# Loading queries, keys and values uncast, casting them on GpSimd, and a values' copy in DRAM ordered by place within the chunk

## The chip, the cores and the metric

The kernel runs on one core of one Trainium2 chip. The metric is the device time of one execution in microseconds (us). TensorE is called PE, VectorE DVE, ScalarE ACT, GpSimd POOL and SyncE SP. POOL, SP and ACT also issue DMAs; all DMAs run on the same 16 engines.

## The reference

Two layers follow each other. The first is chunked attention over four batches of eight heads, 768 places and 64 columns; every chunk of 32 queries sees eight memory places and a span of 16 places before, 32 of and 8 after the chunk:

```python
for c in range(nc):
    l_start, r_end = max(0, c_start - 16), min(S, c_end + 8)
    k_full = np.concatenate([mem_k, k[:, :, l_start:r_end]], axis=2)
    v_full = np.concatenate([mem_v, v[:, :, l_start:r_end]], axis=2)
    scores = scale * np.matmul(q_c, k_full.transpose(0, 1, 3, 2))
    out[:, :, c_start:c_end] = np.matmul(softmax(scores), v_full)
```

The second is a mixture of eight experts over the 3072 rows of 512 columns: `logits + noise_scale * noise` picks two experts for each row, and the output is the weighted sum of `relu(x @ w1[e]) @ w2[e]` over these two.

## The kernel before, in words

**Attention.** A batch is 768 places, six groups of 128; a tile `t` is two groups, so there are three tiles to a batch and twelve in all (`NT`). The main loop runs over tiles `i`. Its engines' orders are written out by hand for PE, ACT, DVE and SP (`manual_schedule`); POOL's heavy instructions are held in program order by `pin`. For each tile the loop does: `scores(i+1)` (PE, L314), then DVE's maximum and subtraction (L340, L342); `turn_p(i)` (PE transposes the weights, ACT copies them, L351); `keep_x(i-1)` (ACT issues the store of a finished tile to DRAM, L405); `turn_x(i-1)` and `gate(i-1)` (L385, L394: the router's logits); `values(i)` (L360); `exps` on ACT (L345). `route` (L207) is a generator: it picks each row's two experts and their place in lists of rows by pair of experts, and its pieces are strewn over the loop, one batch behind; the last batch's routes stand after the loop (L480 to L495).

**Prefetch.** `load_nat` (L108) loads keys, values or queries of one batch with a DMA issued by POOL that casts fp32 to bf16 on its way. `turn` (L302) transposes keys or queries on PE, four units each; ACT and DVE copy them out (L425, L449, L466). Queries of the next batch are turned at the top of the last tile of a batch, keys in the tile before. Values are laid out by two POOL copies (`spread_v`, L284), written to DRAM in order of place, and read back as spans of the chunks (`window_v`, L290: SP issues one write, four reads in runs of 512 bytes and two copies of the memory's values). `await_v` (L416) is a POOL instruction that reads one value of the spans: whatever POOL issues next, the next batch's loads first of all, waits for the spans.

The large buffers of this stage (`xrow`, `vb`, `vp`, `vn`, `nat`) lie in the upper end of the room of the experts' weights (`scratch`, L96); experts 0 to 2 are loaded from tile 6 on, 3 and 4 after the first gathers.

**Experts.** POOL gathers rows from DRAM by the lists (`gather_x`, L534), PE transposes them (`transposes`, L548), and seventeen steps of `mm1` and `mm2` follow (L564, L579), a step for each expert and block of lists. Results are scattered to the output by POOL (`put`, L539).

The framework orders dependent instructions by semaphores. DMAs of SP and ACT share eight of them in turn: a DMA that takes one waits until the last DMA that used it has landed.

## Time and profile before

| | us |
|---|---|
| median of three runs | 411.07 |
| lowest and highest | 406.02, 411.64 |
| the profiled execution: its time | 413.39 |
| its span | 411.4 |
| PE busy | 314.9 (77%) |
| DVE busy | 174.5 (42%) |
| ACT busy | 120.3 (29%) |
| POOL busy | 102.6 (25%) |
| first use of values of batch 0 | 33.83 |
| spans landed, batches 0 to 3 (`await_v`) | 33.89, 67.75, 101.54, 133.80 |
| queries turned, batches 1 to 3 | 51.01, 86.05, 119.21 |
| first gather issued | 174.44 |
| first matmul of the experts | 184.28 |

Times of instructions are from the start of the span. Lines of the order of time give start and length in us, the engine, the line, operation, what is written and read with its shape, and in brackets how long the engine was idle before and what ended that; "issue" there means that nothing in the profile ended it. Lines of the waits give who waited for whom: us in total, how often, the longest. The slices cut the span in 40 equal parts and give busy tenths; PEclk is the granted clock of PE in tenths.

### The profile page before, as it was taken

The numbers are of one execution on the slowest core, as the hardware profiler recorded it, in microseconds if no ns is written. First come the engines' busy times: TensorE is split into PE (matmuls) and PEld (weight loads), VectorE is DVE, ScalarE is ACT, GpSimd is POOL, SyncE is SP. The second block draws the span as 40 slices with busy tenths as digits, with TensorE's granted clock in tenths as the row PEclk, the third lists the DMA queues.
The fourth block names the chain that finished last, engine by engine and source line by source line (L and its number), as shares of the span: only waits on it lengthen the run. The fifth ranks groups of instructions, "written<-read, shape, count | busy, mean of one in ns | idle before, by whom it ended". The sixth has DMA issues, their size and how long they took to land.

```text
span 411.4 us, 8936 instructions
## 1 busy us (share of the span) xinstructions
PE 314.9 (77%) x3841; PEld 203.2 (49%) x3862; DVE 174.5 (42%) x403; ACT 120.3 (29%) x182; POOL 102.6 (25%) x129
## 2 busy tenths in 40 slices
PE   1565394857748563149999999999999999999980
PEld 1444383746636453025555446665446765545530
DVE  1454053759767388832123321594321333112230
ACT  1222342523533332003432234312234222223300
POOL 5202202020120400074516532162250122100040
PEclk9999855555665555558999999999999999989996
DMA  9999994987999999739999970712130011100020
GB/s 129 206 142 102 197 180 71 221 191 116 191 195 157 158 218 222 124 91 177 191 196 246 238 172 14 116 42 90 48 92 1 23 65 45 48 1 3 19 79 31
DMA packets 50093, 49.85 MB, mean 121 GB/s; under 512 B 7064, under 2 KB 42968, under 8 KB 50049
## 3 DMA queue, kind: packets, MB, share of 16 engines
q0 software_dynamic: 28800, 36.32, 46.9%
q1 hardware_dynamic: 14112, 9.90, 12.2%
q10 hardware_dynamic: 7136, 3.02, 3.4%
q8 instruction: 32, 0.52, 0.5%
q14 instruction: 13, 0.10, 0.1%
HBM read 62.00 MB, written 13.96 MB: 185 GB/s over the span
## 4 chain that ended last, share of the span: by engine, by line
PE 52%; DVE 4%; issue 2%; POOL 1%; DMA 1%; POOLq 0%; ACT 0%
PE p_h L573 26%; PE p_y L582 24%; PE p_xt L554 1%; POOL xt L536 1%; DMA xt<-xd,main_src 1%; DVE vals L273 1%; DVE w_all L381 0%; PE p_list L277 0%; DVE facts L254 0%; DVE c L225 0%; DVE c L226 0%; POOLq L767 0%; DVE y L588 0%; DVE ii L227 0%; DVE mm L223 0%
## 5 line engine op out<-in xcount | busy, mean ns | idle before, releaser
L582 PE MATMUL p_y<-w_all,h 128*128 128x512 bf16 (+1 forms) x447 | 102.9, 382 | 1.1 <-issue 0.2
L573 PE MATMUL p_h<-xTt,w_all 128*128 128x384 bf16 (+2 forms) x636 | 102.3, 319 | 0.2
L573 PEld LDWEIGHTS <-w_all 128*128 128x128 bf16 (+1 forms) x704 | 68.3, 99 | 41.9 <-issue 2.7
L561 ACT ACTIVATE h<-p_h 128x512 bf16<-128x512 f32 (+1 forms) x82 | 44.7, 545 | 110.1 <-PE p_h L573 103.9
L559 DVE TENSOR_SCALAR h<-p_h 128x512 bf16<-128x512 f32 (+1 forms) x50 | 31.3, 626 | 93.8 <-PE p_h L573 79.3
L582 PEld LDWEIGHTS <-h 128*128 128x128 bf16 x464 | 45.2, 98 | 52.1 <-issue 1.7
L540 POOL DMA_INDIRECT out_dram<-y,main_dst x28 | 31.0, 1106 | 103.6 <-DVE y L588 89.3
L308 PE MATMUL p_t<-identb,w_all 128*64 128x128 bf16 x384 | 23.0, 313 | 27.8 <-DMA w_all<-in_q_dram 18.6
L588 DVE SCALAR_TENSOR_TENSOR y<-p_y,main_w,y 128x512 f32<-128x512 f32 x28 | 21.0, 750 | 37.4 <-PE p_y L582 32.3
L308 PEld LDWEIGHTS <-w_all 128*64 128x64 bf16 x384 | 20.5, 172 | 29.4 <-DMA w_all<-in_q_dram 19.2
L536 POOL DMA_INDIRECT xt<-xd,main_src x28 | 27.3, 975 | 29.4 <-PE p_xt L554 21.8
L330 PE MATMUL ps_s<-kT,qT 64*32 64x56 bf16 x768 | 24.1, 222 | 10.0 <-issue 10.0
L586 ACT ACTIVATE y<-p_y,main_w 128x512 f32<-128x512 f32 x28 | 19.2, 687 | 41.3 <-PE p_y L582 39.2
L357 ACT COPY pT<-p_p 128x1024 bf16<-128x1024 bf16 x12 | 12.1, 1012 | 50.9 <-PE p_p L354 50.9
L286 POOL COPY w_all<-w_all 128x1536 bf16<-128x1536 bf16 x8 | 11.5, 1466 | 39.0 <-DMA w_all<-in_v_dram 39.0
L323 PE MATMUL ps_s<-mkT,qT 64*128 64x8 bf16 x192 | 18.0, 185 | 2.9 <-DVE sc L342 2.9
L340 DVE TENSOR_REDUCE mx<-ps_s 128x16 f32<-128x1024 f32 x12 | 14.7, 1223 | 10.1 <-PE ps_s L330 9.8
L381 DVE TENSOR_TENSOR w_all<-ps_o,rs 128x512 bf16<-128x512 f32 x24 | 15.5, 686 | 5.9 <-PE ps_o L373 4.9
L417 POOL COPY seen<-w_all 128x1 bf16<-128x1 bf16 x4 | 0.8, 192 | 67.2 <-DMA w_all<-vd 67.2
L323 PEld LDWEIGHTS <-qT 64*128 64x128 bf16 x192 | 10.0, 101 | 13.3 <-issue 5.3
L554 PE MATMUL p_xt<-identb,xt 128*128 128x128 bf16 x116 | 10.6, 237 | 7.4 <-DMA xt<-xd,main_src 7.4
L373 PE MATMUL ps_o<-w_all,pT 64*32 64x64 bf16 x768 | 9.6, 229 | 7.8 <-issue 4.7
(156 smaller groups left out, 297.4 us busy)
## 6 DMA issues: line engine op xcount, KB each, us to landing
w_all<-in_moe_w_dram POOLq DMA_DIRECT2D x12, 1024.0 KB, 16.3
w_all<-in_moe_w_dram POOLq DMA_DIRECT2D x8, 512.0 KB, 7.9
w_all<-in_k_dram POOLq DMA_DIRECT2D x4, 768.0 KB, 8.3
w_all<-in_v_dram POOLq DMA_DIRECT2D x4, 768.0 KB, 12.0
w_all<-in_q_dram POOLq DMA_DIRECT2D x4, 768.0 KB, 15.1
vd<-w_all SPq DMA_DIRECT2D x4, 768.0 KB, 3.4
w_all<-vd SPq DMA_DIRECT2D x8, 384.0 KB, 8.8
xd<-w_all ACTq DMA_DIRECT2D x11, 256.0 KB, 6.6
```

The costliest lines, as they stand in the source:

```text
L308: nc.tensor.transpose(out=p_t[par * 64:par * 64 + 64, s, :], in_=src[:, 2 * pair + par, s * D:(s + 1) * D], identity=identb, tile_position ...
L323: nc.tensor.matmul(out=ps_s[:, par, j, pair, 0:NM], lhsT=q_[rows, pair, tk:tk + 128], rhs=mkT[rows, pair, b * NM:(b + 1) * NM], start=True ...
L330: nc.tensor.matmul(out=ps_s[r * CH:(r + 1) * CH, par, j, pair, NM:KW], lhsT=q_[rows, pair, tr:tr + CH], rhs=k_[rows, pair, tr:tr + WIN], s ...
L381: nc.vector.tensor_tensor(out=xr[:, j, 0:Dm].rearrange("p (c a d) -> p a c d", c=HP, a=2), in0=ps_o[:, :, j], in1=bc(rs[:, j].rearrange("p ...
L536: pin(nc.gpsimd.indirect_dma_start(out=xts[key].bitcast(I32), out_offset=None, in_=xd, in_offset=bass.IndirectOffsetOnAxis(ap=ix, axis=0)))
L540: i = nc.gpsimd.indirect_dma_start(out=out, out_offset=bass.IndirectOffsetOnAxis(ap=ix, axis=0), in_=y, in_offset=None, bounds_check=N - 1 ...
L559: nc.vector.tensor_scalar(out=out_, in0=in_, scalar1=0.0, scalar2=None, op0=Alu.max)
L561: nc.scalar.activation(out=out_, in_=in_, func=Act.Relu)
L573: nc.tensor.matmul(out=o, lhsT=w(kp * F + f * 128, 128), rhs=x[:, kp], start=(kp == 0), stop=(kp == KP - 1))
L582: nc.tensor.matmul(out=p, lhsT=h[:, (f * n + j) * 128:(f * n + j + 1) * 128], rhs=w(KP * F + f * Dm, Dm), start=(f == 0), stop=(f == FB - 1))
L586: nc.scalar.activation(out=y, in_=p, func=Act.Copy, scale=weight)
L588: nc.vector.scalar_tensor_tensor(out=y, in0=p, scalar=weight, in1=y, op0=Alu.mult, op1=Alu.add)
```

## The change

Queries, keys and values are loaded as fp32 (`fetch`), for the first batch by SP and for the others by POOL, and cast by copies: of batch 0 on ACT (keys), POOL and DVE (values) and DVE (queries), of later batches on POOL (`narrow`, `spread_v`). The values' copy in DRAM has one row for each place within the chunk, and in it all 24 chunks and a chunk of zeros on each side; it is written by eight DMAs (`away_v`), and a span is read by six DMAs in which each partition reads one run of 12 KB. `ahead(b)` puts a batch's casts, copies and the loads of the batch after in one sequence on POOL and SP, one batch earlier than before; `await_v` stays for batch 0 and the last. The copies of later batches' queries are all ACT's. The first small loads move from SP to ACT. `xrow` becomes three buffers of a tile. In the last two routes the chain of differences `d` runs on POOL, and the order of the pieces changes; `decode` moves into the hand-written part. The first expert starts after three gathered tiles; the other three are transposed behind its `mm1`.

```diff
-    xrow = [scratch(SO * Dm).rearrange("p (s r) -> p s r", s=SO) for _ in range(2)]
+    xrow = [scratch(2 * Dm).rearrange("p (s r) -> p s r", s=2) for _ in range(3)]
...
+    SV = 8
+    PV = S // SV
+    vp = scratch(H * SV * D)[0:PV]
+    k32, q32 = [scratch(2 * H * SO * D).bitcast(F32).rearrange("p (h c) -> p h c", h=H) for _ in range(2)]
+    v32 = scratch(2 * H * SV * D)[0:PV].bitcast(F32).rearrange("p (h c) -> p h c", h=H)
+    vd = [tc.dram_tile([2, CH, NCH + 2, HP * D], BF16, name=f"vd{i}") for i in range(2)]
+
+    def fetch(eng, x, b):
+        t, a, n = {"k": (k32, k, SO), "q": (q32, q, SO), "v": (v32, v, SV)}[x]
+        i = eng.dma_start(out=t, in_=a[b].rearrange("h (p s) d -> p h (s d)", s=n))
+        if eng is nc.gpsimd:
+            pin(i)
+
+    for x in "kvq":
+        fetch(nc.sync, x, 0)
...
     for i in range(2):
-        for r0, n in ((0, LC), (LC + S, CH - LC)):
-            nc.sync.dma_start(out=vd[i][r0:r0 + n, :], in_=zeros[0:n, :])
+        for x in range(2):
+            nc.scalar.dma_start(out=vd[i][x].rearrange("k c w -> k c w")[:, 0:NCH + 2:NCH + 1, :], in_=zeros[:, x])
-    nc.sync.dma_start(out=mks, in_=mem_k.rearrange("b h m d -> (b h m) d").rearrange("(x p) d -> p x d", p=128))
+    nc.scalar.dma_start(out=mks, in_=mem_k.rearrange("b h m d -> (b h m) d").rearrange("(x p) d -> p x d", p=128))
...
-    def route(g0, n, lg):
+    def route(g0, n, lg, eng=nc.vector):
...
-        nc.vector.tensor_tensor(out=d, in0=mm[:, 1], in1=mm[:, 0], op=Alu.subtract)
+        hold = pin if eng is nc.gpsimd else lambda m: m
+        hold(eng.tensor_tensor(out=d, in0=mm[:, 1], in1=mm[:, 0], op=Alu.subtract))
         for i in range(3):
-            nc.vector.tensor_copy(f_[:, :, 2 + i], d)
+            hold(eng.tensor_copy(f_[:, :, 2 + i], d))
...
+    def spread_v(engs=(nc.gpsimd, nc.gpsimd)):
+        for par, eng in enumerate(engs):
+            i = eng.tensor_copy(
+                out=vp.rearrange("p (s a c d) -> p a c s d", s=SV, a=2, c=HP)[:, par],
+                in_=v32.rearrange("p (c a) (s d) -> p a c s d", a=2, s=SV)[:, par])
...
+    def away_v(b):
+        src = vp.rearrange("p (s a w) -> p s a w", s=SV, a=2)
         for par in range(2):
+            for r in range(CH // SV):
+                nc.sync.dma_start(out=vd[b % 2][par, r * SV:(r + 1) * SV, 1:NCH + 1, :].rearrange("s c w -> c s w"),
+                                  in_=src[r:PV:CH // SV, :, par, :])
 
     def window_v(b):
         t, o = vb[b % 2], vd[b % 2]
-        nc.sync.dma_start(out=o[LC:LC + S, :].rearrange("(p s) c -> p (s c)", s=SO), in_=vp)
         for par in range(2):
...
+            for r0, n, c0, k0 in ((0, LC, 0, CH - LC), (LC, CH, 1, 0), (LC + CH, RC, 2, 0)):
+                nc.sync.dma_start(out=t[p0 + NM + r0:p0 + NM + r0 + n], in_=o[par, k0:k0 + n, c0:c0 + NCH, :])
             nc.sync.dma_start(out=t[p0:p0 + NM], in_=mvn[b * NM:(b + 1) * NM, cols].unsqueeze(1).to_broadcast([NM, NCH, 256]))
-            for r0, n in ((0, CH), (CH, WIN - CH)):
-                nc.sync.dma_start(out=t[p0 + NM + r0:p0 + NM + r0 + n],
-                                  in_=o[r0:r0 + S, cols].rearrange("(c k) w -> k c w", k=CH)[0:n])
+
+    def narrow(x, b):
+        pin(nc.gpsimd.tensor_copy(nat[b % 2][x], (k32, q32)[x]))
...
+    def ahead(b):
+        if b < B:
+            narrow(0, b)
+            if b + 1 < B:
+                fetch(nc.gpsimd, "k", b + 1)
+            spread_v()
+            away_v(b)
+            if b + 1 < B:
+                fetch(nc.gpsimd, "v", b + 1)
+            narrow(1, b)
+            if b + 1 < B:
+                fetch(nc.gpsimd, "q", b + 1)
...
-        spread_v(0)
+        for h in range(0, H, 4):
+            nc.scalar.copy(nat[0][0][:, h:h + 4], k32[:, h:h + 4])
+        fetch(nc.gpsimd, "k", 1)
+        spread_v((nc.gpsimd, nc.vector))
+        away_v(0)
         window_v(0)
+        for u in range(HP):
+            o_, i_ = turn(0, u)
+            nc.scalar.copy(o_, i_)
+        for h in range(0, H, 4):
+            nc.vector.tensor_copy(nat[0][1][:, h:h + 4], q32[:, h:h + 4])
         await_v(0)
-        for u in range(2 * HP):
+        fetch(nc.gpsimd, "v", 1)
+        fetch(nc.gpsimd, "q", 1)
+        for u in range(HP, 2 * HP):
...
         pbs[0] = exps(scores(0))
         nc.scalar.dma_start(out=nz, in_=moe_noise.rearrange("(g p) e -> p g e", p=128))
+        ahead(1)
         for i in range(NT):
             if tp == 0 and b + 1 < B:
                 window_v(b + 1)
-                await_v(b + 1)
-                if b + 2 < B:
-                    load_nat(nat[b % 2][0], k, b + 2)
-                    load_nat(vn, v, b + 2)
-                    load_nat(nat[b % 2][1], q, b + 2)
-                    spread_v(b + 2)
+                if b + 1 == B - 1:
+                    await_v(b + 1)
+                ahead(b + 2)
...
-                    (nc.scalar.copy if u % 2 else nc.vector.tensor_copy)(o_, i_)
+                    nc.scalar.copy(o_, i_)
...
-        ra = route(g0, SO - 2, lgs[B - 1][:, 0:SO - 2])
-        rb = route(g0 + SO - 2, 2, lgs[B - 1][:, SO - 2:SO])
+        ra = route(g0, SO - 2, lgs[B - 1][:, 0:SO - 2], nc.gpsimd)
+        rb = route(g0 + SO - 2, 2, lgs[B - 1][:, SO - 2:SO], nc.gpsimd)
...
-    for i in range(3):
-        turn_block(0, i)
+    turn_block(0, 0)
+    transposes(xTs[0], 2, blocks[0][0][2:3])
     dst, wl = next(dec)
...
         h = mm1(xTs[b][:, :, s0:s0 + (n - 1) * ds_ + 1:ds_, :], n, static_w(e), i % 2)
+        if i == 0:
+            transposes(xTs[0], 3, blocks[0][0][3:4])
+            turn_block(0, 2)
```

## The prediction

> **What bounds the kernel now.** I read the slices first, then the waits, then the order of time around one batch, then the chain.
>
> ```profile
> ## 2 busy tenths in 40 slices
> PE   1565394857748563149999999999999999999980
> PEclk9999855555665555558999999999999999989996
> DMA  9999994987999999739999970712130011100020
> ```
>
> Two stages stand here. From slice 18 (about 184 us) on, TensorE is at 9 with the clock near full: the mixture of experts, 216 us, bound by PE; among its waits from 184 to 400 us PE shows 0.2 us in all. The change leaves its matmuls alone. The first 184 us, attention, have PE at half busy and DMA at 9. So the question is what PE waits for there.
>
> ```profile
> POOL seen L417 <- DMA w_all<-vd: 67.2, 4, 17.7
> POOL w_all L286 <- DMA w_all<-in_v_dram: 39.0, 4, 11.3
> PE p_t L308 <- DMA w_all<-in_q_dram: 18.6, 4, 6.3
> PE ps_s L330 <- issue: 10.0, 2, 5.7
> ```
>
> GpSimd (POOL) holds the prefetch: it waits 67.2 us for the spans of the values, and only behind that issues the next batch's loads. PE pays with waits for queries. The order of time around batch 0 to 1 shows the loop:
>
> ```profile
> 33.83 0.73 PE L373 MATMUL ps_o<-w_all,pT 64*32 64x64 bf16 x63 [3.04 <-DMA w_all<-vd]
> 33.89 0.19 POOL L417 COPY seen<-w_all 128x1 bf16<-128x1 bf16 x1 [17.23 <-DMA w_all<-vd]
> 34.35 0.92 POOL L109 DMA_DIRECT2D w_all<-in_k_dram  x1 [0.26 <-issue]
> 41.63 2.77 PE L308 MATMUL p_t<-identb,w_all 128*64 128x128 bf16 x48 [1.55 <-DMA w_all<-in_k_dram]
> 47.16 2.87 POOL L286 COPY w_all<-w_all 128x1536 bf16<-128x1536 bf16 x2 [10.12 <-DMA w_all<-in_v_dram]
> 51.01 2.77 PE L308 MATMUL p_t<-identb,w_all 128*64 128x128 bf16 x48 [6.29 <-DMA w_all<-in_q_dram]
> 67.78 0.24 PE L330 MATMUL ps_s<-kT,qT 64*32 64x56 bf16 x6 [5.67 <-issue]
> 82.34 1.37 DVE L256 TENSOR_TENSOR d<-d,facts 128x6 f32<-128x6 f32 x1
> ...
> 85.18 0.17 DVE L256 TENSOR_TENSOR d<-d,facts 128x6 f32<-128x6 f32 x1
> ```
>
> The reader is to see: spans of batch 0 land at 33.8, loads go out at 34.35, keys are used 7.3 us, values 12.8 us, queries 16.7 us later. PE loses 6.29 us for the queries of batch 1, and 4.10 and 4.86 for those of batches 2 and 3 (at 86.05 and 119.21). The 5.67 us at 67.78 have no releaser and end as the span reads land (`seen` at 67.75); such a stall of 4.32 stands at 143.25. During plain loads it is smaller: 1.08 at 77.99.
>
> **The change part by part.** In the built program I followed which instruction waits for which. Durations are of the profiled execution (span 411.4, time 413.39, which is 2.3 above the median of the three runs, 411.07).
>
> 1. First batch, to the first use of values (33.83 before). The three loads go out on SP at about 0.8 in place of 1.35 on POOL, and land about 4.1 apart as before (9.50, 13.79, 17.62): keys 8.5 to 9, values 13. An uncast load is not in the trace; nearest rows: 3.4 us to landing for the uncast 768 KB `vd<-w_all`, and twice that, 6.8, for its 1536 KB; I take the cast load's 4.1 to 5.5, since it reads the same bytes. New: the small loads moved to ACT stand there ahead of the keys' cast, and one waits for the keys' landing: five issues of about 0.45 (rows of 0.37 to 0.54), then two ACT copies of 128x1536. 128x768 took 0.80 and 128x1024 1.01, so 1.43 each (bounds 1.01 and 2.0): done at 14. Then POOL issues keys of batch 1, which share the engines with the queries: queries at 20, keys(1) at 23. Queries are cast on DVE in two halves, 0.84 each by the two cast rows (128x128 0.25, 32x512 0.41; upper bound 1.6); PE turns them from 21, where before it was 17.62. The scores follow as before, so `exps(0)` starts 8.1 to 8.3 later, at 29.5 (25.70 before).
> The first of the eight copies of values to DRAM waits for keys(1), since the build holds it behind every uncast load ahead of it. It goes at 23, eight issues of 0.5 (rows 0.35 to 0.86), landed by 30; this is hidden, because in the middle of the span reads SP stands still: the copy of `mvn` there uses the semaphore of the noise load and waits for it, and ACT issues that load with `exps(0)` at 29.5. Its landing no row shows: between 2.8 (the gate's noise load) and 8.8 (a span read); I take 5, being 96 KB of short runs. Then five more issues (2.9) and 2.3 to land: 39.6. So the spans are there at 39.6, not 33.8: **+5.8**.
>
> 2. From there to the queries of batch 1 (17.1 us before). POOL order now: wait for spans, load v(1), load q(1), cast k(1), load k(2), two value casts, load v(2), cast q(1). The copies to DRAM wait for k(2), and v(2) waits for all eight copies; cast q(1) is queued behind v(2). So: three loads 17.5 (16.7 before, k(2) issued later); eight issues 4.0 (bounds 2.8 and 6.9); landing 2.5 (row 3.4 with its transfer); load issue 0.9; cast 2 x 1.44 = 2.9 by L286's 2.87 for the same 3072 elements (fp32 in place of bf16; up to 5.8); semaphores 0.4. 28.2, **+11.1**. PE turns these queries at 67.7, not 51.0: **+16.9** there. PE is then idle about 17 us, against 6.29.
>
> 3. What the later batches gain. Span reads in 12 KB runs queue less; I take both issue stalls down to the 1.08 seen during loads: **-4.6** and **-3.2** (bounds 0 and all). Queries(2) need k(3), eight copies and a cast behind them: ready near 97.4, when PE would be ready at 94; wait 3.3 for 4.10, and 0.89 of PE waiting for ACT's copy goes: **-1.7**. Queries(3) have no such copy ahead of their cast and come 10 us early: **-5.7** (4.86 and 0.89). Copies of queries moved from DVE to ACT cost nothing: PE turned keys with all four on ACT in 2.77 without a stall.
> Casts on POOL delay DVE: the operation at 82.34 took 1.37 while L286 ran, its like at 85.18, after it, 0.17. Two to five casts can meet `route`'s small operations: between 0 and 13 us, mostly while PE waits for queries anyhow; I take **+1.0**.
>
> 4. Tail. `route`'s d chain moves to POOL, whose queue holds only the six weight issues (4.9 us from 133.92, long done by 162.9): 12 operations of 0.15 to 0.18 leave DVE, in part covered by the PE wait beside them: **-1.0** (0 to 2.2). The first expert starts after three gathered tiles instead of six: third transposed by 180.5, matmuls at 181 not 184.28; twelve transposes then move behind it, 0.7: **-2.5** (bounds 0 and 3.2). Hidden: xrow of three buffers (a store lands in 6.6, three tiles last over 17), earlier scratch reuse by expert weights (they took 134 to 170, needed from 184), `decode` moved.
>
> Sum: 16.9 - 4.6 - 3.2 - 1.7 - 5.7 + 1.0 - 3.5 = -0.8. The profiled execution would take 412.6; against the median, 411.07 - 0.8 = 410.3.
>
> [...] From 90 to 103 us PE had no gap over 1.1 us and its granted clock stayed 0.50. [...]
>
> **The rivals.**
> Faster: the start-up chain is shorter than I make it. If uncast loads take 3.4 each, like the copy to DRAM, and the noise load doesn't hold SP, spans land at 35 and queries(1) come 22 later, at 57: +6 in place of +16.9, and the sum is -11.7, 399. For it: the spans are 112 runs of 12 KB in place of 2688 of 512 bytes (shapes of L298). Against it: 16.7 us for three loads was read-bound in the trace at the same bytes. It decides once queries(1) come before about 60.
> Slower, by loads: an uncast load writes twice the bytes; at 6.8 each the three loads take 21 to 23, keys(1) delay the start by 2 to 3, and queries(2) wait some 5 longer since k(3) gates them too: +11 to +13, 422. For it: the DMA row is at 9 throughout the first 18 slices. It decides once three loads take over 21 us after the spans.
> Slower, by the casts: each of the five POOL casts that can meet `route` holds a DVE operation to its end, on the path: 2.9+2.9+2.0+2.0+2.9, +11.7 over my 1.0, 422. [...] The trace agrees (1.37 and 1.40 for 0.17). Against it on the path: both hits before fell while PE waited for queries.
> The issue stalls stay as they are: +7.8, 418, still within 2%.
>
> **How the numbers follow.** Within 2% is 402.8 to 419.3, about what a measurement of this kernel can tell from no change. The forecast has 0.50 (0.12 of it for stalls that stay, 0.08 for the clock), and its own range is 403 to 418: the first step 3 either way by the noise load's bounds, the second 3 by the issues', the stalls up to 7.8. The short start-up has 0.31, slower by loads 0.13, by casts 0.06. I take a third of the faster case to lie below 397 and under half of the slower ones over 421, so 397 to 421 leaves out under 2 in 10. The time is that of the forecast, 410.3.
>
> **What would show it.** Spans' first use at 39.6 and an SP wait for noise: step 1. Queries(1) turned near 67.7, POOL's load of v(2) waiting for the copies to DRAM: step 2; if PE turns them before 60, that step is wrong. Stalls without a releaser under 2 us in the scores, waits for queries(2) and (3) of 3.3 and 0: step 3. A first `p_h` matmul after three gathers: step 4. The forecast falls if uncast loads are not 4 to 5.5 us, or if `route` on DVE stretches on PE's path.

## The result, and the profile after

The changed kernel takes 440.88 us (median of 4 executions, 440.37 to 441.12) beside 411.36 for the kernel before, measured with it (406.02 to 415.75). The ratio is 1.0763, with a 95% interval of 1.0661 to 1.0864: slower by 7.6%. Executions of before differ by up to 10 us: the ratio leaves out its slowest (415.75), and its profiled one took 413.39. The prediction was 410.3, its range 397 to 421. The profiled execution of the changed kernel spans 439.1 us, 27.7 more than the 411.4 of before.

The slices come first:

```profile
PE   0243250256674969522999999999999999999970
PEclk9999995565655575555799999999999999999995
DMA  8948495899698676999699997162121011100020
```

From slice 19 (about 209 us) on the stage of the experts looks as before. The loss is ahead of it. Of the first ten slices PE is at 2 or less in 0, 1, 4, 6 and 7, and DMA, which before stood at 9 in most slices of attention (4 in slice 6), is at 4 to 6 in several. DMA is not fuller than before. It waits too. The waits say for what (in total us, times, longest):

```profile
POOL seen L457 <- DMA w_all<-mvn: 56.6, 2, 34.7
...
POOL w_all L114 <- DMA vd<-w_all: 28.8, 2, 15.1
PE p_t L325 <- POOL w_all L316: 28.8, 2, 24.0
...
PE ps_o L390 <- issue: 16.1, 4, 7.3
```

The second and third line are one chain: the load of values(b+1) waits on POOL for the copies away, the cast of queries(b) stands behind it, and PE waits for the cast. The order of time through the first two batches (start, duration, instruction, idle time before it and what ended it):

```profile
25.14 6.57 SPq L303 DMA_DIRECT2D vd<-w_all  x8
31.83 1.27 SPq L312 DMA_DIRECT2D w_all<-vd  x3
40.89 0.76 SPq L313 DMA_DIRECT2D w_all<-mvn  x1
...
52.45 0.73 PE L390 MATMUL ps_o<-w_all,pT 64*32 64x64 bf16 x63 [6.29 <-DMA w_all<-mvn]
...
73.13 6.44 SPq L303 DMA_DIRECT2D vd<-w_all  x8
...
81.82 0.79 POOL L114 DMA_DIRECT2D w_all<-in_v_dram  x1 [15.11 <-DMA vd<-w_all]
82.60 2.75 POOL L316 CAST w_all<-w_all 128x3072 bf16<-128x3072 f32 x1
...
85.41 2.77 PE L325 MATMUL p_t<-identb,w_all 128*64 128x128 bf16 x48 [23.96 <-POOL w_all L316]
```

The reader is to see the hole of SP between 33.1 and 40.89, in the middle of the first span reads (its waits give 7.8 us for the noise load `nz`), and PE idle for 24 us until 85.41. The table sets the same points of both kernels side by side, from the orders of time; the points of the experiments follow below in the same columns.

| point | before | after | later by |
|---|---|---|---|
| first copies of values away, issued | 16.69 | 25.14 | 8.5 |
| first values on PE (spans of batch 0 there) | 33.83 | 52.45 | 18.6 |
| second copies away, issued | 50.06 | 73.13 | 23.1 |
| queries(1) turned on PE | 51.01 | 85.41 | 34.4 |
| last values on PE | 154.87 | 184.78 | 29.9 |
| first matmul of the experts | 184.07 | 209.96 | 25.9 |
| end of the span | 411.4 | 439.1 | 27.7 |

All that is lost is lost by queries(1). After that the batches come at the pace of before (copies away at 73.13, 110.40 and 142.37; before at 50.06, 85.14 and 118.01).

### The profile page after: what moved, and what is told of

Read it like the earlier page. It is cut to its first block, busy times and chain, and to the rows that moved or that the text cites. A ratio compares the mean times of both kernels' runs of the same rounds, so it can differ in the third digit from the quotient of the medians.

```text
span 439.1 us, 9020 instructions
## 1 busy us (share of the span) xinstructions
PE 310.4 (71%) x3862; PEld 199.8 (46%) x3862; DVE 167.5 (38%) x387; ACT 128.5 (29%) x192; POOL 121.5 (28%) x141
## 3 DMA queue, kind: packets, MB, share of 16 engines
q1 hardware_dynamic: 12032, 14.42, 15.6%
## 4 chain that ended last, share of the span: by engine, by line
PE 50%; DVE 3%; DMA 1%; POOL 1%; issue 0%; POOLq 0%; ACT 0%
PE p_h L608 25%; PE p_y L617 23%; PE p_xt L589 2%; DMA xt<-xd,main_src 1%; POOL xt L571 0%; DVE vals L280 0%; DVE w_all L398 0%; PE p_list L284 0%; DVE c L232 0%; DVE c L231 0%; POOLq L806 0%; DVE y L623 0%; DVE ii L233 0%; DVE mm L229 0%; DVE oh_l L278 0%
## 5 line engine op out<-in xcount | busy, mean ns | idle before, releaser
L325 PE MATMUL p_t<-identb,w_all 128*64 128x128 bf16 x384 | 20.4, 291 | 40.1 <-POOL w_all L316 28.8
L325 PEld LDWEIGHTS <-w_all 128*64 128x64 bf16 x384 | 18.4, 159 | 41.2 <-POOL w_all L316 28.9
L293 POOL CAST w_all<-w_all 96x2048 bf16<-96x2048 f32 x7 | 14.1, 2044 | 27.9 <-DMA w_all<-in_v_dram 27.9
L390 PEld LDWEIGHTS <-pT 64*32 64x32 bf16 x768 | 7.5, 105 | 23.1 <-issue 23.0
L508 ACT COPY qT<-p_t 128x768 bf16<-128x768 bf16 x12 | 8.8, 805 | 28.5 <-PE p_t L325 28.4
## 6 DMA issues: line engine op xcount, KB each, us to landing
w_all<-in_moe_w_dram POOLq DMA_DIRECT2D x12, 1024.0 KB, 16.2
```

What stands on the lines that cost most here:

```text
L325: nc.tensor.transpose(out=p_t[par * 64:par * 64 + 64, s, :], in_=src[:, 2 * pair + par, s * D:(s + 1) * D], identity=identb, tile_position ...
L390: nc.tensor.matmul(out=ps_o[r * CH:(r + 1) * CH, par, j, pair, :], lhsT=pT[rows, j * HP + pair, r * CH:(r + 1) * CH], rhs=vb[b % 2][rows, ...
```

## The experiments

The first theory was the chain just read: SP stops for the noise load, the reads in 12 KB runs land late, and the cast of queries(1) is stuck behind the copies. Its rivals were that the uncast loads are too much to move, and that the new order of the values' copy is slow by itself. The points of time of all runs, in us of the profiled executions (time is the median of all executions; first values are those that need both halves of the spans; the kernel before, run beside each group of experiments, had medians between 409.63 and 414.74, so times of different groups compare to about 1%, and the ratio is the better measure there):

| run | time | ratio to before (95%) | first values | queries(1) | first values of batch 1 | last values |
|---|---|---|---|---|---|---|
| before | 411.36 | 1 | 33.83 | 51.01 | 70.46 | 154.87 |
| after | 440.88 | 1.0763 (1.0661 to 1.0864) | 52.45 | 85.41 | 107.05 | 184.78 |
| e1 | 442.36 | 1.0777 (1.0663 to 1.0892) | 53.41 | 72.67 | 106.39 | 184.33 |
| e2 | 440.17 | 1.0743 (1.0595 to 1.0891) | 49.23 | 82.19 | 103.58 | 179.88 |
| e3 | 445.81 | 1.0848 (1.0706 to 1.0990) | 54.32 | 87.32 | 113.36 | 189.00 |
| e4 | 444.14 | 1.0798 (1.0648 to 1.0949) | 52.80 | 85.73 | 107.30 | 187.15 |
| e5 | 442.28 | 1.0715 (1.0582 to 1.0848) | 50.74 | 70.07 | 113.25 | 186.85 |
| e6 | 438.20 | 1.0625 (1.0495 to 1.0754) | 43.19 | 62.23 | 104.95 | 182.53 |
| e7 | 439.45 | 1.0680 (1.0545 to 1.0816) | 42.29 | 99.40 | 113.30 | 183.49 |
| e8 | 421.87 | 1.0239 (1.0114 to 1.0364) | 38.90 | 55.84 | 90.78 | 164.89 |
| e9 | 430.04 | 1.0398 (1.0343 to 1.0452) | 39.65 | 62.55 | 81.46 | 172.30 |
| e10 | 411.98 | 0.9960 (0.9907 to 1.0012) | 34.27 | 55.13 | 71.79 | 154.97 |
| e11 | 422.42 | 1.0180 (1.0101 to 1.0259) | 38.81 | 56.02 | 74.65 | 166.13 |
| e12 | 409.99 | 0.9906 (0.9850 to 0.9961) | 33.12 | 50.38 | 68.47 | 153.94 |
| e13 | 430.28 | 1.0541 (1.0460 to 1.0623) | 39.80 | 62.75 | 78.74 | 171.24 |
| e14 | 438.37 | no interval | 40.81 | 63.86 | 80.76 | 175.97 |
| e15 | 404.72 | 0.9861 (0.9803 to 0.9918) | 34.98 | 48.76 | 65.94 | 150.29 |
| e16 | 441.44 | 1.0815 (1.0725 to 1.0905) | 42.31 | 68.08 | 88.17 | 181.53 |
| e17 | 428.21 | 1.0483 (1.0389 to 1.0576) | 35.91 | 85.04 | 98.56 | 173.51 |
| e18 | 454.76 | 1.1074 (1.0954 to 1.1193) | 46.79 | 72.93 | 93.97 | 198.50 |

### The waits that the profile names, one by one

**e1: the cast of queries ahead of the load that waits.**

```diff
             spread_v()
+            narrow(1, b)
             away_v(b)
             if b + 1 < B:
                 fetch(nc.gpsimd, "v", b + 1)
-            narrow(1, b)
-            if b + 1 < B:
                 fetch(nc.gpsimd, "q", b + 1)
```

> The cast of queries(b) stands on POOL ahead of the issue of values(b+1), which waits for the eight copies away; nothing else is changed. Theory of the queue (POOL holds the cast of queries(1) at 82.60 although its load has landed with keys(2) by 73): the cast runs at about 73 to 76, queries(1) turn at about 76 instead of 85.41, the wait of 4.79 for queries(2) goes too, and the time is 427 to 432 (-9 to -14). Rival, the volume of the loads: the three uncast loads, 1.5 MB each, are what is late, the wait moves to the next of them, and the time is 438 to 441.

The wait was there and goes: queries(1) turn at 72.67, 12.7 us earlier. The time does not move (442.36). PE's own line says where the gain went:

```profile
72.67 2.77 PE L325 MATMUL p_t<-identb,w_all 128*64 128x128 bf16 x48 [10.00 <-POOL w_all L316]
...
106.39 0.74 PE L390 MATMUL ps_o<-w_all,pT 64*32 64x64 bf16 x63 [15.04 <-DMA w_all<-mvn]
```

Behind the wait for queries stood another of nearly the same end: the spans of batch 1 land at 106.39, where the changed kernel uses them at 107.05. The longest wait of PE was a cover over the chain of the values (load, spread, copies away, span reads), and that chain sets the pace.

**e2: the noise load issued at the start.**

```diff
     nz = const.tile([128, NG, E], F32, name="nz")
+    nc.scalar.dma_start(out=nz, in_=moe_noise.rearrange("(g p) e -> p g e", p=128))
...
-        nc.scalar.dma_start(out=nz, in_=moe_noise.rearrange("(g p) e -> p g e", p=128))
```

> The noise load is issued at the start, behind the memory keys and the gate's weights, instead of behind exps(0); nothing else is changed. Theory of the wait on SP (7.8 us in the middle of the first span reads): the second half of the reads is issued at about 34 instead of 41.76, the first values come at 44 to 46 instead of 52.45, and the time is 433 to 435. Rival, the reads themselves are slow, as 12 KB runs that land in 7 us: both halves run together and land at 49 or later, and the time is 437 to 441.

SP no longer stops, and the first values come 3.2 us earlier, at 49.23, not at 44 to 46. The rival holds: with nothing between them the reads, issued from 33.38 on, still take 15.9 us to the first use. Before, in runs of 512 bytes, they took 13.8 (20.06 to 33.83).

**e3: the same reads in runs of 512 bytes**, by padding each place's row.

```diff
-    vd = [tc.dram_tile([2, CH, NCH + 2, HP * D], BF16, name=f"vd{i}") for i in range(2)]
+    vd = [tc.dram_tile([2, CH, NCH + 2, HP * D + 32], BF16, name=f"vd{i}")[:, :, :, 0:HP * D] for i in range(2)]
```

> The values' DRAM copy keeps its order, but each place's row of chunks is padded by 32 elements, so that the same span reads go in runs of 512 bytes instead of 12 KB. Theory that the long runs are what lands late (45.21 to 52.45, about 7 us where before took 2.3): the last reads land in 2.5 to 3 us, the first values come at about 48, and the time is 435 to 437. Rival, the landing is the queue's and the volume's and not the run length's: no change, 440 to 441, or slower, 442 to 446, since the reads are 24 times as many packets.

445.81: the rival's slower side. The run length is not what lands late. The 2.3 of the theory stands in no row of before, either: there the first values were used 9.55 us after the last read was issued.

```profile
21.99 2.29 SPq L298 DMA_DIRECT2D w_all<-vd  x2
```

**e4: the small loads ahead of the three first loads in the program.**

```diff
-    for x in "kvq":
-        fetch(nc.sync, x, 0)
...
     nc.scalar.dma_start(out=wgs[:, :, E:2 * E], in_=moe_w_noise.rearrange("(kp p) e -> p kp e", p=128))
+    for x in "kvq":
+        fetch(nc.sync, x, 0)
```

> The small loads (zeros, memory keys and values, gate weights) stand ahead of the three first loads in the program, so that the load of queries(0) no longer waits for the memory keys; nothing else is changed. Theory that this wait (queries(0) issued at 12.10 instead of about 1.9) sets the start: copies away at about 20 to 22 instead of 25.14, queries(0) turned at about 20 instead of 25.65, the noise load 5 earlier, and the time is 434 to 437. Rival, the first 25 us are bound by the 6 MB of four uncast loads: copies still at 25, and the time is 439 to 441.

This run doesn't tell. The queries' load still went out at 12.01, so the wait that it was to remove stayed. What that wait costs is open.

### Which part of the change costs

**e5 and e6: the copies away without partition steps.** The eight copies read every fourth partition, and in the built program such a read waits for all three uncast loads ahead of it (SP's waits ahead of the copies of the changed kernel: 52.4 us in three stops for keys, 16.8 in two for queries, 14.3 in one for values). e5 keeps eight copies but reads neighbouring partitions; e6 makes one copy of each half.

```diff
-            for r in range(CH // SV):
-                nc.sync.dma_start(out=vd[b % 2][par, r * SV:(r + 1) * SV, 1:NCH + 1, :].rearrange("s c w -> c s w"),
-                                  in_=src[r:PV:CH // SV, :, par, :])
+            nc.sync.dma_start(out=vd[b % 2][par, :, 1:NCH + 1, :].rearrange("(r s) c w -> c r s w", s=SV),
+                              in_=src[:, :, par, :])
```

(This is e6; e5 has four of them in each half, over six chunks each.)

> Still eight copies away of the same bytes to the same places, but each reads 24 neighbouring partitions (six whole chunks) instead of every fourth partition. In the program the copies then wait only for the spread, no longer for the three uncast loads, and the load of values(b+1) waits only for the spread of values(b), no longer for the landing of the eight copies. Theory of these two waits as the loop that sets the pace (copies 73.13, values(2) issued 81.82, spread of it 101.82, copies 110.40): copies(1) go at about 67, values(2) is issued at about 67, queries(1) turn at about 73 instead of 85.41, copies(2) at about 90 instead of 110.40, and the time is 410 to 422. Rival, the volume of the uncast loads sets the pace whatever waits for what: 430 to 438. The first values stay at about 52 by both, since the noise load still stops SP.

> One copy away for each half, over all 96 partitions, instead of four: the same bytes and places, two issues instead of eight, and none of the waits named for the eight copies of whole rows. Theory of the waits and of the issue time (8 copies 6.4 to 7.4 us of SP): another 2 to 5 us below the eight copies of whole rows, 406 to 420. Rival, one copy lands later than four beside one another: the same as the eight or up to 5 us above.

Everything up to queries(1) comes earlier, in e6 by 23 us (62.23), and by the last values 2 us of it are left. Both times lie above what their theories allow, and e5's above its rival's too. Again the spans of batch 1 are late, at 104.95 in e6. SP's waits in e6:

```profile
SPq L311 <- DMA vd<-w_all: 46.6, 4, 16.8
...
SPq L311 <- DMA xd<-w_all: 23.7, 3, 8.9
```

Two things are in it. The span reads wait 46.6 us for the copies to land: freed from the loads, the copies now run beside three loads in flight, and what was issued at 55.74 has landed only at 75.11. And 23.7 us go to a transfer that the reads don't need, the store of finished rows `xd`. The DMAs of SP and ACT take eight semaphores in turn (in the trace of the changed kernel their issues carry the numbers 101 to 108, round and round), and here a read's number is one that a row store still holds. The changed kernel stops 0.9 us for `xd`. In e5 such stops sum to 21.4 us. So the theory that the waits of the copies set the pace falls: without them the copies meet the loads.

**e7 and e8: half of the change each, loads as early as in the changed kernel.** e7 has the casting loads of before with the new order; e8 the old order (one copy away, `mvn` ahead, two reads a half) with the fp32 loads and GpSimd's casts.

```diff
-        t, a, n = {"k": (k32, k, SO), "q": (q32, q, SO), "v": (v32, v, SV)}[x]
+        t, a, n = {"k": (nat[b % 2][0], k, SO), "q": (nat[b % 2][1], q, SO), "v": (v32, v, SV)}[x]
...
     def narrow(x, b):
-        pin(nc.gpsimd.tensor_copy(nat[b % 2][x], (k32, q32)[x]))
+        pass
```

```diff
+        nc.sync.dma_start(out=vd[b % 2][LC:LC + S, :].rearrange("(p s) c -> p (s c)", s=SV), in_=vp)
...
+            for r0, n in ((0, CH), (CH, WIN - CH)):
+                nc.sync.dma_start(out=t[p0 + NM + r0:p0 + NM + r0 + n],
+                                  in_=o[r0:r0 + S, cols].rearrange("(c k) w -> k c w", k=CH)[0:n])
```

> The order of the values' copy, the spans and the edits at the end are kept; the loads are again the casting ones on POOL, straight into the bf16 tiles, and the casts of keys and queries are gone. In the program the eight copies then wait for the spread alone, and so does the load of values(b+1). Theory of the waits: the loop of copies and loads is gone with them, 408 to 422, though the first spans still stop for the noise. Rival, the order of the copy (12 KB reads, eight copies, SP stopped) is what costs: 425 to 440.

> The loads in fp32, the casts on GpSimd and the edits at the end are kept; the values' copy in DRAM and the span reads are those of before (one copy away, runs of 512 bytes). In the program the copy away then waits for the spread alone and the load of values(b+1) likewise. Theory of the waits: 405 to 420. Rival, the uncast loads and their casts are what costs: 430 to 440.

e8 gives back 19.0 of the 29.5 us with the fp32 loads and casts still there. So the uncast loads are not the main cost; 421.87 is just above the range of its theory. e7 does not tell: it loads keys and queries of batch 3 over those of batch 1 before these are turned (there are two tiles, and the changed kernel had the fp32 tiles between), so batch 1 is computed with the wrong keys and queries, and PE waits for the later load.

**e9 to e12: four kernels of one design.** In all four the three loads of a batch are issued only behind POOL's wait for the spans of the batch before, as in the kernel before. This gate was dropped by the change for two of the batches.

```diff
-                if b + 1 == B - 1:
-                    await_v(b + 1)
+                await_v(b + 1)
+                for x in "kvq" if b + 2 < B else "":
+                    fetch(nc.gpsimd, x, b + 2)
                 ahead(b + 2)
```

The loads in `ahead` go, and keys(1) are loaded behind the first wait as well.

e9 has the new order (two copies) and fp32 loads, e10 the old order and fp32 loads, e11 the new order and casting loads, e12 the old order and casting loads.

> The new order with the two copies away, fp32 loads and casts, and now all three loads of a batch are issued only behind POOL's wait for the spans of the batch before, as before (keys(1) too, which had been issued at 13.6). Theory that the transfers hold one another up (with three 1.5 MB loads in flight the two copies of the second batch took 17 and 27 us to land, where the first ones took 6): the copies land in 5 to 7 us and the spans in 14 to 16, one batch takes 34 to 38 us, the last values come at 165 to 172 instead of 183 to 185, and the time is 420 to 427. Rival, the new order or the volume costs this time whatever is in flight: last values at 180 or later, 434 to 442.

> The old order of the values' copy and the old reads, with the fp32 loads, the casts on GpSimd and the edits at the end, and all three loads of a batch behind the wait for the spans, as before. Theory that transfers hold one another up: without loads in flight the copy lands in 3.5 and the reads in 14, and only the longer loads and the casts are left, 2 to 5 us a batch: last values at 158 to 168 and the time 412 to 422, not above the ungated one (421.9). Rival, early loads are a gain and the gate costs: 424 to 432.

> The new order with two copies away, casting loads as before and the same gate: of the change there are left only the order of the values' copy, the 12 KB runs and the edits at the end. Theory that the runs bring nothing (first reads 14 us in runs of 512 bytes before, 15 in runs of 12 KB with the noise load out of the way) and two copies with six reads cost 3 to 6 us a batch: last values at 165 to 178 and 418 to 430. Rival, the long runs are a gain once nothing disturbs them: 400 to 410.

> Old order, casting loads, the same gate: of the change there are left the edits at the end (part of the last routing on GpSimd, the first expert behind three gathers), half of the first spread on VectorE, and the copies of turned keys and queries on ScalarE. Both theories: last values within 2 us of before (155.4), 2 to 4 us less from there to the end, 406 to 411; above 414 would say that these small edits cost by themselves.

e11 and e12 came out as their theories had it, e10 at the lower end of its range and e9 3 us above its own, below the rival's.

| us | old order | new order |
|---|---|---|
| casting loads, gated | 409.99 (e12) | 422.42 (e11) |
| fp32 loads and casts, gated | 411.98 (e10) | 430.04 (e9) |
| fp32 loads and casts, early | 421.87 (e8) | 438.20 (e6) |

The new order costs 12 to 18 us in each row. The fp32 loads with their casts cost 2 in the old order and 8 in the new. Loads issued early cost 10 and 8 (2.8 and 2.3% by the ratios, since these are two groups). Stops of SP for the row stores are in three of the six: 29.6 us in all in e11, 23.7 in e6 and 10.3 in e8, so that neither e11's time nor the last row is the order or the loads alone. e9, e10 and e12 have none ahead of their copies and reads, and the 18 us between e9 and e10 are the cleanest of these differences. That early loads hold up the copy by themselves is read in e8: the reads wait 20.2 us in three stops for the copy to land (first line), where in e10 they wait 9.5 in four (second).

```profile
SPq L309 <- DMA vd<-w_all: 20.2, 3, 7.8
SPq L309 <- DMA vd<-w_all: 9.5, 4, 3.1
```

Why the order costs is read from one batch of e10 (first) and of e9, cut into loads with spread, copy away, and span reads (columns: window, length, then the busy time of PE, weight loads, DVE, ACT and POOL, granted clock, DMA share, GB/s):

```profile
34.40:51.20 16.80, 8.93 (x287) 7.60 (x276) 5.50 (x9) 5.79 (x7) 8.71 (x7) 1.00 0.83 298
51.20:54.60 3.40, 0.00 (x0) 0.00 (x0) 0.00 (x0) 0.00 (x0) 2.28 (x1) 0.58 0.64 244
54.60:67.40 12.80, 9.96 (x298) 8.14 (x299) 4.17 (x7) 5.89 (x7) 0.47 (x1) 0.63 0.84 144
```

```profile
39.70:57.50 17.80, 9.03 (x287) 7.71 (x286) 5.50 (x9) 5.79 (x7) 7.62 (x7) 1.00 0.91 267
57.50:61.90 4.40, 0.00 (x0) 0.00 (x0) 0.00 (x0) 0.00 (x0) 4.00 (x3) 1.00 0.64 184
61.90:77.50 15.60, 10.99 (x298) 8.96 (x299) 4.17 (x7) 5.82 (x7) 0.59 (x1) 1.00 0.77 135
```

Each link of the chain is longer in the new order. The cut between copy and reads is where the reads begin, and in e9 they begin when the first of the two copies has landed: by the packet records the second lands at 63.52, 1.65 us into the window of the reads. Cut at the last packet of the copies, the three batches of each kernel read:

| us | e10 | e9 | longer, in all |
|---|---|---|---|
| spans there to first copy issued | 16.9, 16.5, 16.9 | 17.9, 19.4, 20.0 | 7.1 |
| to the copies' last packet | 2.9, 4.0, 3.0 | 6.0, 6.1, 6.0 | 8.2 |
| to the next spans | 13.3, 12.5, 13.1 | 14.0, 14.4, 14.9 | 4.4 |

So the copies, twice as long, cost most, and the reads least. In the loads and the spread the two orders differ as well: values come on 96 partitions, and the two spreads take 3.73 us where 2.88. From `seen` to `seen` a batch takes 33.1, 33.0 and 32.9 in e10 and 37.8, 39.9 and 40.9 in e9. In the changed kernel the copies are worse still; this is its second set, of eight:

```profile
73.10:79.70 6.60, 0.00 (x0) 0.00 (x0) 0.00 (x0) 0.00 (x0) 0.00 (x0) 0.50 0.38 96
```

96 GB/s for 6.6 us where the window of e10's one copy shows 244 for 3.4. Each of the eight takes 0.8 us of SP to issue, and by the packet records hardly anything is in flight when the next begins.

### Inside the new order

**e13: `mvn` ahead of the span reads again**, on e9.

```diff
+            nc.sync.dma_start(out=t[p0:p0 + NM], in_=mvn[b * NM:(b + 1) * NM, cols].unsqueeze(1).to_broadcast([NM, NCH, 256]))
             for r0, n, c0, k0 in ((0, LC, 0, CH - LC), (LC, CH, 1, 0), (LC + CH, RC, 2, 0)):
                 nc.sync.dma_start(out=t[p0 + NM + r0:p0 + NM + r0 + n], in_=o[par, k0:k0 + n, c0:c0 + NCH, :])
-            nc.sync.dma_start(out=t[p0:p0 + NM], in_=mvn[b * NM:(b + 1) * NM, cols].unsqueeze(1).to_broadcast([NM, NCH, 256]))
```

> New order, two copies, fp32 loads, gated (430.0), and the read of the memory values stands again ahead of the span reads of its half, so that its 512-byte packets run while the copies land. Theory that this read, put last by the change, is what lands late (issued at 68.51, landed at 77.50): from the copies' issue to the landing 17 us instead of 20, 3 to 4 us in each of four batches, 414 to 420. Rival, the 12 KB reads are themselves the last: the wait moves to them and the time is 426 to 431.

430.28, in the rival's range: no gain. The wait only changes its name, from `mvn` to the span reads:

```profile
POOL seen L456 <- DMA w_all<-vd: 68.6, 4, 21.6
```

**e14: e9 with the pad of e3.**

> New order, two copies, fp32 loads, gated (430.0), with each place's row of chunks padded by 32 elements, so that the same reads go in runs of 512 bytes. Theory that the run length is neither gain nor loss (12 KB packets took about 1.05 us, 11.7 bytes a ns, 512-byte ones of the same reads before 45 ns, 11.4): 427 to 433. Rival A, the long runs are a gain that the rest hides: 434 to 440. Rival B, the long runs are the loss of the new order: 418 to 425.

Its four executions spread from 433.39 to 444.36, and the lower two (433.39 and 435.70) stand where the range of the theory meets that of rival A, so the time does not decide. The profile does: from the first read's issue to the spans it takes 17.8, 17.4 and 17.5 us in the first three batches, e9 16.7, 15.6 and 16.0. Within the new order the long runs gain 1 to 2 us a batch, which is less than the order costs; rival B falls.

**e16: e9 with each span read cut into two of 12 chunks**, so that the runs are 6 KB.

```diff
-                nc.sync.dma_start(out=t[p0 + NM + r0:p0 + NM + r0 + n], in_=o[par, k0:k0 + n, c0:c0 + NCH, :])
+                for x in range(0, NCH, NCH // 2):
+                    nc.sync.dma_start(out=t[p0 + NM + r0:p0 + NM + r0 + n, x:x + NCH // 2],
+                                      in_=o[par, k0:k0 + n, c0 + x:c0 + x + NCH // 2, :])
```

> New order, two copies, fp32 loads, gated (430.0), each span read issued as two over half the chunks, so that the runs are 6 KB and a place's row can go through two engines. Theory that few long packets leave engines unevenly loaded (reads of 8 and 16 rows make 8 and 16 packets for 16 engines): the reads land 1 to 2 us earlier a batch, 423 to 427. Rival, bytes a ns of an engine in these reads are what counts, whatever the run: 428 to 433, the six issues more a batch included.

441.44, which neither theory allows. SP's waits say why it doesn't tell: with the number of DMAs changed, the reads stop 13.4 us for row stores and 7.3 for the noise load, which e9's reads do not. Whether shorter runs would spread better stays open.

### Loads in flight, and the whole changed kernel

**e17: e12 without the gate.** Edits as e7's with the old order.

> Old order, casting loads, the edits at the end, and the loads issued as early as the changed kernel issues them, not behind the wait for the spans (with it: 410.0). Theory that loads in flight hold up the copy and the reads whatever their kind: the copies of the second and third batch land 10 us or more after their issue, and the time is 417 to 424. Rival, this happens with the fp32 loads alone, and early casting loads are free or a gain: 403 to 412.

428.21, more than the theory allows, and it has the fault of e7: queries and keys of batch 3 come over those of batch 1, which is computed with the wrong ones. PE waits 31.51 us at 73.67 for just that later load. So it says nothing of early casting loads.

**e18: the changed kernel, with the gate alone.**

> The changed kernel with one thing undone: the three loads of a batch are issued only behind POOL's wait for the spans of the batch before. Theory that the parts add up (gate 8 in the new order, two copies instead of eight 3): 431 to 436, with the copies landing within 3 us of the last issue. Rival, the eight copies wait for the loads anyway, so that the gate only puts the loads later: 438 to 446.

454.76, above what either theory allows: the gate that won 8 us with two copies loses 14 with eight. The parts do not add up. The eight copies wait for all three loads, so with the gate nothing overlaps (47.50 to 70.2 the loads, to 76.9 the copies, to 94.0 the reads), and SP stops again where it needn't:

```profile
SPq L312 <- DMA xd<-w_all: 21.4, 3, 7.5
...
SPq L312 <- DMA nz<-in_moe_noise_dram: 9.0, 1, 9.0
```

In the changed kernel itself the stop for the rows is 0.9 us in all, so the 14 us are the gate and these stops together, and no run parts them.

**e15: the version that the others point to.** e12, with values as the first of the three first loads and both reads of `mvn` issued while the copy lands.

```diff
-    for x in "kvq":
+    for x in "vkq":
         fetch(nc.gpsimd, x, 0)
...
             nc.sync.dma_start(out=t[p0:p0 + NM], in_=mvn[b * NM:(b + 1) * NM, cols].unsqueeze(1).to_broadcast([NM, NCH, 256]))
+        for par in range(2):
+            p0 = par * 64
+            cols = slice(par * 256, (par + 1) * 256)
             for r0, n in ((0, CH), (CH, WIN - CH)):
```

> Old order, casting loads, gated, the edits at the end (410.0), and two things more: values are the first of the three first loads, and both reads of the memory values are issued while the copy is landing, ahead of all span reads. Theory that the chain of values (load, spread, copy, reads) sets the pace and that each read less behind the copy counts: first values 3 to 5 us earlier, 1 us a batch after it, 402 to 407. Rival, what goes earlier meets the loads of keys and queries in flight and lands when it did: 409 to 411.

404.72, ratio 0.9861 (0.9803 to 0.9918): 1.4% below the kernel before. The first spans land at 30.65 against 33.17 in e12. PE gains nothing from that, since keys and queries come later (first values 34.98), but the loop of loads starts 2.5 us sooner and queries(1) are turned at 48.76 against 50.38. From the copy's issue to the spans it is no shorter than in e12 (17.0, 16.4 and 16.3 against 17.4, 16.2 and 15.9), so the reads of `mvn` were no cost, and the theory's 1 us a batch is not there. How much of the gain is new against e12 is open: the two ran in different groups, the intervals of their ratios overlap, and the profiles differ by 3.65 us at the last values.

## Why the prediction was wrong, step by step

The kinds of wait were right, the order of time among them too, and nearly every size was too small. Beside the sum of -0.8 stand +27.7: of the 28.5 between them, 12.8 are in step 1, 4.7 in step 2, 9.7 in step 3 and 1.3 in step 4.

**Step 1, the first values: +5.8 predicted, +18.6 measured.** This failed most. The chain was the predicted one, noise load and all. Its terms: `exps(0)` and with it the noise load came at 33.73, not 29.5 (+4.2), since the queries' load was itself held on SP until 12.10, by a semaphore shared with the memory keys (10.2 us in SP's waits); the prediction had all three loads go out at about 0.8. The noise load held SP until 40.89, 7.2 after its issue where 5 was taken (+2.2). The five issues behind it took 4.3, not 2.9 (+1.4). And the last reads landed 7.2 after their issue, not 2.3 (+4.9). For that 2.3 the prediction names no row, and the row of before says 9.55 (24.28, when the last read had been issued, to 33.83). Long runs land 1 to 2 us a batch sooner than short ones of the same order (e14), which is far from that factor, and from the copies' last packet to the spans the new order takes 14.0 us in e9 where the old takes 13.3 in e10. The gated kernels split the loss in another way: first values at 34.27 with the old order (e10), 39.65 with the new (e9), 46.79 with eight copies (e18), 52.45 with keys(1) loaded early as well.

**Step 2, to queries(1): +11.1 predicted, +15.8 measured.** The queue on POOL was as predicted. Loads took 20.6 instead of 17.5 until the copies could go, the eight issues 6.44 instead of 4.0; landing, load issue and cast were within 0.3. What failed is what the step was for. It took queries(1) as the point that PE's path hangs on; e1 takes the wait away and the time stays, because the spans of batch 1 end at the same place. The chain of the values was costed only for batch 0.

**Step 3, the later batches: -14.2 predicted, -4.5 measured** (103.86 from queries(1) to the last values before, 99.37 after). Queries(3) came without a wait, as predicted; queries(2) waited 4.79, not 3.3. The stalls without a releaser did not shrink:

```profile
97.08 0.59 PE L390 MATMUL ps_o<-w_all,pT 64*32 64x64 bf16 x46 [4.09 <-issue]
104.37 0.24 PE L347 MATMUL ps_s<-kT,qT 64*32 64x56 bf16 x6 [4.01 <-issue]
```

There are two more, of 3.61 and 2.29. The prediction laid them to the span reads, and took 7.8 us off for reads in long runs; that such reads queue less, no run shows. The trace gives another reading. Counted through PE's records in order of time (weight loads, matmuls, semaphores), all five stalls of over 1 us without a releaser in the attention of before stand at places (from 0) that leave 193 when divided by 256 (1729, 2241, 3521, 4545, 4801), and so do those of the changed kernel (1473, 1729, 2753, 3009, 4801), of e9 and of e10. (The 7.29 us ahead of 45.95 are another matter: PE stands there at an instruction that waits for the semaphores of a span read and of the first `mvn` read, and the latter's last update is at 45.86.) And within each of the four stalls, or just ahead of it, runs one packet of 16,384 bytes of the queue that the profile names `instruction` (starts at 93.72, 101.73, 132.14 and 139.13, lengths 1.70, 1.20, 1.33 and 1.10 us), as one does in the stalls of before (64.88, 1.39 us long, in the one that ended at 67.78). The author's inference is that PE waits there for its own next 256 instructions, and not for the spans; no run tests it. The profiled executions of both kernels have 32 such packets each, and why only a few of them go with a stall is not shown; no run took a stall away.

**Step 4, the end: -3.5 predicted, -2.2 measured** (from the last values to the end of the span 256.5 before, 254.3 after; e12, which has these edits without the loads and the order, 254.3 too). The first matmul of the experts came 4.0 sooner after the last values, and 1.8 went back behind it, where the prediction had 0.7.

The rivals: slower by loads had the right sign with 422, and its condition, three loads of over 21 us, was just missed (20.6). What the prediction gave for it, a DMA row at 9 throughout the first 18 slices, the row does not show (4 in slice 6, 3 in slice 17). And e10 shows that the uncast loads are not the cause of most of it. That the casting loads were read-bound is an inference of the prediction; measured is that with fp32 written in place of bf16 e10 takes 16.9, 16.5 and 16.9 us from the spans to the first copy, and the kernel before 16.2, 17.4 and 16.5. Slower by casts did not happen: one operation of `route` was held (3.30 us at 119.49, for 0.17 unheld), while PE waited for queries(2) until 122.81. The short start-up fell with the noise load, which did hold SP. For the 0.08 that the prediction gives to the clock, no run shows a gain: in the kernel before, the granted clock was 0.50 from 90 to 103 us, where PE had no gap over 1.1 us, and 0.77 in the mean of one iteration of the loop (100.84 to 106.36). That the new order is slower by itself was no rival at all: its reads stood in the sum as a gain, 7.8 us of stalls.

What stays open: why loads and spread take longer in the new order (7.1 us in three batches, of which the spread's own time explains less than half), and why reads that come back from DRAM move so slowly in either form.

## What to carry to other kernels

Before counting on a removed wait, find the wait that ends next behind it, for every batch and not for the first alone: here queries(1) could come 12.7 us earlier for nothing. Transfers of one chain (load, copy out, read back) are judged by how long the chain takes with its neighbours in flight; a gate that keeps bulk loads from running beside the short copies was worth 8 to 10 us with one or two copies a batch, though not with eight that waited for the loads anyway, and longer runs were no substitute for it. Where DMAs take a few semaphores in turn, as the eight here, read the issuing queue's waits again after each edit that changes the number of DMAs in a loop or their time: stops for row stores were 0.9 us in the changed kernel, 23.7 in e6 and 21.4 in e18.

## What the runs showed of the hardware

In the read back from DRAM, long runs moved hardly faster than short ones. In the trace's packet records the 12,288-byte packets of e9's second batch take 1.12 us each (11 bytes a ns), the 512-byte ones of e10 49 ns in the median (10 bytes a ns), while e10's copy away moved its 6,144-byte packets in 242 ns (25 bytes a ns) and the fp32 loads of keys and queries their 4,608 bytes in 0.20 us (23). The values' loads on 96 partitions, in packets of 4,096 bytes, took 0.25 us each in e9 (16).

How many packets ran at once went with the rows. In e10 the copy of 128 partitions has 16 to 17 packets in flight; in e9 the copies, over 24 chunks, mostly have 9 to 13 (12 in the median), and the reads have 15 to 17 while rows of 16 and 32 are read but only 8 of the long packets for 3.2 us at their end (70.4 to 73.6), which fits the reads of 8 rows and what is queued ahead of them. The semaphores in the trace of the changed kernel show like counts around its first span reads: a copy over 24 chunks lands with 12 updates (31.59 to 31.76), the reads of 16 and of 32 rows with 16 each (34.75 to 35.45 and 36.73 to 38.65), the read of 8 rows with 8 (38.95 to 39.35). Which engines the packets went through the records do not say. That the smaller counts are what makes copies and reads longer is not shown either: no run changed the rows alone.

The stalls of PE in step 3 go with two measured figures: their places, which lie multiples of 256 apart, and one packet of 16,384 bytes of the `instruction` queue each. In this attention stage four stalls of the changed kernel (4.09, 4.01, 3.61 and 2.29 us, 14.0 in all) have such a packet within them or just ahead. That PE waits for the packet is inferred from this and not tested.
